# Attention and a state-space layer side by side: loads, masks, the skip term and the flag rearranged

## The chip, the cores and the metric

The kernel runs on one core of a Trainium2 chip. Five engines work beside each other: TensorE (matrix products), VectorE, ScalarE (written ACT), GpSimd and SyncE (SP), and DMA queues move data. The metric is the time of one execution on the device in microseconds; less is better.

## The reference

Two layers work on sequences of 2048 positions of width 448, and their outputs stand side by side in the result.

- Layer A is attention with 16 heads of width 28. Position s sees itself and seven earlier positions at distances 2, 4, ..., 14:

```
qkv    = x @ wqkv                              # q, k, v: 16 heads of 28
idx    = pos[:, None] - arange(8) * 2          # masked where idx < 0
attn   = softmax(q . k[idx] * 28**-0.5)
a      = (attn . v[idx]) @ wo
```

- Layer B is a linear recurrence with a complex diagonal of 448 entries:

```
dt = exp(log_dt);  Lam_bar = exp(dt * Lam)
B_bar = ((Lam_bar - 1) / Lam)[:, None] * (B_re + i B_im)
h[t] = Lam_bar * h[t-1] + B_bar @ x[t]
y[t] = 2 * real(C @ h[t]) + x[t] * Dskip
out  = concatenate([a, y], axis=-1)            # bf16, 1 x 2048 x 896
```

The term `x * Dskip` is called the skip term below.

## The kernel before

**Two positions as one.** All distances in layer A are even, so even and odd positions never meet. The kernel reads both inputs as 1024 pairs of width 896, transposed on the way in (`xA`, `xB`: pieces of 128 pairs, the helper `xbar_x`, lines 277 and 278). Layer B is also run on pairs: the scan has 1024 steps, and the odd and the even output of a pair are two products.

**Loads.** Lines 284 to 303 issue the loads. SP issues the transposing loads of x and then those of B. ACT issues the three parts of `wqkv`: V into `Wv`, K and Q into `Wraw`, each in a part of 384 rows and a tail of 64 rows. GpSimd issues the four small vectors of layer B into `rows`. A DMA takes one of eight semaphores in turn, so a ninth load waits on its issuing engine until the load that had its semaphore before has landed.

**Layer A.** `v0` to `v8` (name in the plan) are the projections to V, each in two halves of 4 and 3 pairs of matmuls on the two halves of TensorE's rows (`pair`, line 509). Between the halves stands a tiny memset on GpSimd, the tick (`relay`, line 523): it waits for the first half, and the second half waits for it. `wp` (`n_wp`, line 481) copies K and Q weights into the padded `Wpad`; `q<q><s><c>` are the projections to K and Q in three chunks of positions. `s`, `x`, `a`, `n`, `ot` are scores with mask (`msk`, built on GpSimd by `gms`, lines 324 to 336), exponentials on ACT (line 690), weighted sums of V (line 702), normalization on VectorE (line 709) and a transpose by DMA into `OT`. `w0` to `w7` multiply with `wo` and are stored.

**Layer B.** `tr`, `pA`, `pB`, `e1`, `e2`, `p2`, `p3` compute the small per-entry coefficients from `rows`; `p3` (line 455) is a chain of 26 and more VectorE operations of 128x4 elements that gives the coefficients that scale C. `t0` to `t4` make tables of sines and cosines (`tab`): `t0` and `t1` (line 433) the arguments, `t2` and `t4` the sines on ACT. The exponentials of layer A wait for `t4`. `l1`, `l2`, `wtx` scale B and transpose it by DMA into `WT`; `b<half><k>` multiply with x (line 742); then on VectorE `ma`, `ri`, `sc`, `mb`, `ro`: rotate by the tables, scan, rotate back into the state `h`. `cg`, `ch` scale C into `C1` and `C2`, `g` makes `Gm`. `y0` to `y7` (the even outputs, line 879 and 881) and `z0` to `z7` (the odd outputs, lines 888 to 891) are the output products for 128 pairs each; y4 to y7 need the second half of the scan. The skip term of the even output is inside `Gm` (by the diagonal `dgE`); that of the odd output is four matmuls with the diagonal matrices `dgO` (lines 889 and 891).

**The guard.** The softmax leaves out the maximum. `guard1` to `guard3` (lines 932 to 945) test that every sum stayed within bounds and write `flag`. At the end every engine loads the flag (line 956) and branches (line 958) to `exact_attention`, which runs only if the test fails.

**Order.** Each step above is a node of a plan (class `Plan`, line 33): with the engines that may run it and an estimated cost for each, what it depends on, a rank, and for some an earliest time `at`. `run` is a greedy list schedule on these estimates: an engine that is free takes the ready node of the lowest rank. Ranks come from the table `RANK` (line 27), two numbers for a group: a start and a step per index. The result is a fixed order of instructions on each engine, which the chip then follows, with semaphores between engines. PSUM is held by four units (`unit`), each taken by a product and given back by its eviction (`evac`, line 491, on VectorE or ACT).

Of the kernel before, what the change touches and what calls it, by code (L numbers as in the profile page):

```python
# [7 lines left out]
BF16 = mybir.dt.bfloat16  # L8
# [8 lines left out]
NB = 9  # L17
# [9 lines left out]
RANK = {"v": (-66.31, 15.076), "q0": (294.15, -25.592), "q1": (-315.77, 68.252), "s": (340.5, 1.243), "a": (-235.18, 100.084), "b0": (313.86, 16.665),  # L27
        "b1": (1356.35, 1.953), "d0": (322.12, 89.775), "d1": (1443.2, 48.596), "l": (1449.65, 70.241), "t": (88.82, 72.345), "p3": (-158.67, -158.858),
        "cg": (19.42, -10.986), "ch": (1359.74, -129.532), "g": (444.15, -19.668), "y": (337.07, 51.059), "w": (1219.89, 24.257), "gu": (1542.4, -111.348),
        "q2": (576.66, 87.15), "wp": (286.96, 21.742)}  # L30
# [186 lines left out]
def kernel(  # L217
# [65 lines left out]
    V.memset(zz[:, 0:640], 0.0)  # L283
    xbar_x(xA, xA2, 0, 128)
    ACT.dma_start(Wv[:, 0:3, :], A_wqkv[0:384, 2 * D:3 * D].rearrange("(k p) n -> p k n", p=128))
    ACT.dma_start(Wv[0:64, 3, :], A_wqkv[384:448, 2 * D:3 * D])
    for i, vec in enumerate((B_log_dt, B_Lambda_re, B_Lambda_im, B_Dskip)):
        G.dma_start(rows[7 * i:7 * i + 7, :], vec.rearrange("(c p) -> c p", p=64))
    for i in range(1, 4):
        xbar_x(xA, xA2, 128 * i, 128 * i + 128)  # L290
    for q in (1, 0):
        ACT.dma_start(Wraw[:, 0:3, D * q:D * q + D], A_wqkv[0:384, D * q:D * q + D].rearrange("(k p) n -> p k n", p=128))
        ACT.dma_start(Wraw[0:64, 3, D * q:D * q + D], A_wqkv[384:448, D * q:D * q + D])
    for i in range(4, 8):
        xbar_x(xA, xA2, 128 * i, 128 * i + 128)
# [6 lines left out]
    for i in range(4):  # L302
        xbar_x(xB, xB2, 128 * i, 128 * i + 128)
# [129 lines left out]
    def n_t1(e):  # L433
        for k in range(4):
            kk = tmpB[:, 2560 + 512 * (k % 2):3072 + 512 * (k % 2)]
            V.tensor_scalar(kk, iota, p["f2"][:, k:k + 1], MAGIC, ALU.mult, ALU.add)
            V.scalar_tensor_tensor(ang[:, k, :], kk, -MAGIC, ang[:, k, :], ALU.add, ALU.subtract)  # L437
# [17 lines left out]
    def n_p3(e):  # L455
        q = {k: v[:] for k, v in p.items()}
        ts(q["nr"], q["a1"], -1.0, ALU.add)
        tt(q["den"], lre, lre, ALU.mult); tt(q["t0"], lim, lim, ALU.mult); tt(q["den"], q["den"], q["t0"], ALU.add)
        V.reciprocal(q["rd"], q["den"])
        ts(q["rd"], q["rd"], 2.0, ALU.mult)  # L460
        tt(q["gr"], q["nr"], lre, ALU.mult); tt(q["t0"], q["b1"], lim, ALU.mult)
        tt(q["gr"], q["gr"], q["t0"], ALU.add); tt(q["gr"], q["gr"], q["rd"], ALU.mult)
        tt(q["gi"], q["b1"], lre, ALU.mult); tt(q["t0"], q["nr"], lim, ALU.mult)
        tt(q["gi"], q["gi"], q["t0"], ALU.subtract); tt(q["gi"], q["gi"], q["rd"], ALU.mult)
        tt(q["hr"], q["gr"], q["a1"], ALU.mult); tt(q["t0"], q["gi"], q["b1"], ALU.mult); tt(q["hr"], q["hr"], q["t0"], ALU.subtract)
        tt(q["hi"], q["gr"], q["b1"], ALU.mult); tt(q["t0"], q["gi"], q["a1"], ALU.mult); tt(q["hi"], q["hi"], q["t0"], ALU.add)
        for n in ("g", "h"):
            re, im, sa, pa = q[n + "r"], q[n + "i"], q["s" + n], q["p" + n]
            ts(sa[:, 0:3], re[:, 0:3], 1.0, ALU.mult)
            tt(sa[:, 3:4], re[:, 3:4], sgn[:], ALU.mult)  # L470
            ts(sa[:, 4:7], re[:, 0:3], -1.0, ALU.mult)
            ts(pa[:, 0:4], im[:, 0:4], -1.0, ALU.mult)
            ts(pa[:, 4:7], im[:, 0:3], -1.0, ALU.mult)
# [71 lines left out]
    def halves(name, cost, fn, deps, rank, h, at):  # L545

        x = node(name + "_", {"P": 4 * cost}, lambda e: fn(0), deps, rank, alloc="mm", at=at, mode="h")
        k = node(name + "k", {"G": 0.12}, lambda e: relay(h), [x], -200)
        return x, node(name, {"P": 3 * cost}, lambda e: fn(1), [k], -50, mode="h")
# [4 lines left out]
    late = 17.0  # L554
    gm = []
    for i, f in enumerate(gms):
        gm.append(node(f"gm{i}", {"G": 0.42}, f, gm[-1:], 4, at=late))
# [4 lines left out]
    tr = node("tr", {"P": 0.15}, n_tr, [g_e], 0, alloc="mm", at=7.4)  # L562
# [8 lines left out]
    p3 = node("p3", {"V": 3.45}, n_p3, [p2], ("p3", 0))  # L571
    t0 = node("t0", {"A": 2.4}, n_t0, [pB, g_i], ("t", 0))
    t1 = node("t1", {"V": 4.6}, n_t1, [t0], ("t", 0))
    t2 = node("t2", {"A": 1.9}, n_t2, [t1, e2], ("t", 0))
    t3 = node("t3", {"V": 1.2}, n_t3, [t2], ("t", 0))
    t4 = node("t4", {"A": 2.0}, n_t4, [t3], ("t", 0))
    dg = [node(f"dgO{k}", {"G": 0.5}, lambda e, k=k: g_dgO(e, k), [pD], 15, at=late) for k in range(4)]
    for k in range(4):
        dg.append(node(f"dgE{k}", {"G": 0.5}, lambda e, k=k: g_dgE(e, k), [pD] + gm + dg[4:], 15, at=late))
    vw = node("vw", {"V": 1.0}, n_vw, [], 0, at=5.3)  # L580
    wp = {(q, z): node(f"wp{q}{z}", {"V": 1.55, "A": 2.9}, lambda e, q=q, z=z: n_wp(e, q, z), [g_p], ("wp", 2 * z + 1 - q), at=8.5 if q else 10.0)
# [19 lines left out]
    for i, m in enumerate(MS):  # L601
        h = {}
        l1 = node(f"l1{m}", {"A": 0.58, "V": 0.46}, lambda e, m=m, h=h: n_l1(e, m, h), [p2], ("l", i), alloc="wt", at=16.8)
# [22 lines left out]
    def at_x(t):  # L626
        return (5.9, 6.9, 7.8, 8.9, 10.2, 11.5, 12.8, 14.1)[(t - 1) // 128]
# [104 lines left out]
    for hf in range(2):  # L732
        for k in range(4):
# [45 lines left out]
            def ro(e, k=k, hf=hf, h=h, big=big):  # L779
# [8 lines left out]
                else:  # L788
                    V.tensor_tensor(hb[0:64, 3, to], a[0:64, 0], a[64:128, 1], ALU.subtract)
                    V.tensor_tensor(hb[64:128, 3, to], a[64:128, 0], a[0:64, 1], ALU.add)  # L790
                    if hf == 0:
# [3 lines left out]
                      rb_, alloc="mm", at=22.5)  # L795
# [64 lines left out]
    outv = out[0].rearrange("(t two) n -> t two n", two=2)  # L860
    ny = [0]

    def stage():
        if "ys" not in lazy:
            lazy["ys"] = t_([128, 8, 2, D], BF16, "ys", "rW")
        ny[0] += 1
        return lazy["ys"][:, (ny[0] - 1) % 8]
    for t in range(8):
        tk = slice(128 * t, 128 * t + 128)
        hf = t // 4  # L870
        h = {}

        def pe0(e, t=t, tk=tk, h=h, hf=hf):
            if t == 6:
                tc.mark_branch_hint_location("exact", engines=(mybir.EngineType.PE,))
            ps = h[0] = h[1] = unit()
            hb, lo = hbuf(hf), 128 * (t % 4)
            for m in range(7):
                PE.matmul(ps[:, 0, 0:D], hb[:, m, lo:lo + 128], lazy["C2"][:, m, :], start=(m == 0), stop=False, skip_group_check=True)  # L879
            for k in range(4):  # L880
                PE.matmul(ps[:, 0, 0:D], xB[:, k, tk], Gm[:, k, :], start=False, stop=(k == 3), skip_group_check=True)  # L881

        def pe1(e, t=t, tk=tk, h=h, hf=hf):
            if t == 7:
                h[1] = unit()
            ps, hb, lo = h[1], hbuf(hf), 128 * (t % 4)
            for m in range(7):
                PE.matmul(ps[:, 1, 0:D], hb[:, m, lo + 1:lo + 129], lazy["C1"][:, m, :], start=(m == 0), stop=False, skip_group_check=True)  # L888
            PE.matmul(ps[:, 1, 0:64], xB[:, 3, tk], dgO[:, 0, 0:64], start=False, stop=False, skip_group_check=True)
            for k in range(3):  # L890
                PE.matmul(ps[:, 1, 64 + 128 * k:192 + 128 * k], xB[:, 4 + k, tk], dgO[:, 1 + k, :], start=False, stop=(k == 2), skip_group_check=True)  # L891

        def ev(e, a, b, h=h):
            if "o" not in h:
                h["o"] = stage()
            evac(e, h["o"][:, a:b], h[a][:, a:b, 0:D])

        def st(e, a, b, tk=tk, h=h):
            SP.dma_start(outv[tk, a:b, D:2 * D], h["o"][:, a:b])
        r = ("y", t)  # L900
        hs = [rout[hf, k] for k in range(4)]
        n0 = node(f"y{t}", {"P": 2.0}, pe0, hs + c2 + gn, r, alloc="mm")
        n1 = node(f"z{t}", {"P": 1.57}, pe1, [n0] + c1, (r[0], r[1], -0.1), alloc="mm" if t == 7 else None)
        for a, b in ((0, 1), (1, 2)) if t == 7 else ((0, 2),):
            n2 = node(f"ye{t}{a}", ab((b - a) * D), lambda e, a=a, b=b, ev=ev: ev(e, a, b), [n1 if b == 2 else n0] + qdone, r,
                      frees=[(n1 if a else n0, 0)])
            node(f"yo{t}{a}", {"S": 0.6}, lambda e, a=a, b=b, st=st: st(e, a, b), [n2], 60 + 3 * t, lat=2.2)
    for t in range(8):
        tk = slice(128 * t, 128 * t + 128)
        h = {}  # L910

        def pe(part, tk=tk, h=h):
            if part == 0:
                h["ps"] = unit()
            o, w = OT(), lazy["wo"]
            pair(h, part, h["ps"], D, lambda o_, k: o[o_:o_ + 64, k, tk], lambda o_, k: w[o_:o_ + 64, k, :])

        def ev(e, h=h):
            h["o"] = stage()
            evac(e, h["o"], h["ps"][:, :, 0:D])  # L920
# [69 lines left out]
```

## Time and profile before

| | us |
|---|---|
| median of 7 runs | 138.84 (138.62 to 140.29) |
| profiled execution | 138.76 |
| its span | 136.9 |
| TensorE busy (matmul) | 127.4 |
| VectorE busy | 104.6 |
| ScalarE busy | 93.0 |
| GpSimd busy | 21.5 |

The span runs from the first to the last recorded instruction of the program; the execution is 1.9 us longer. Busy time counts the time in which an engine works, without waits and without issuing DMAs. The page also cuts the span into 40 slices of 3.42 us and gives the busy share of each in tenths. "PE" is TensorE, "PEld" its loading of weights, "DVE" VectorE, "POOL" GpSimd, and a "q" behind a name means the engine's sequencer. In a row of the timeline stand start, length, engine, line, operation, what is written and read, the count, and in brackets how long the engine had been idle and what ended that.

### The profile page before, as it was taken

To read this page: it belongs to the slowest core of one execution; us is meant where nothing else is said; L and a number is where in the kernel's file an instruction comes from. 1 tells how busy PE (TensorE), PEld (TensorE's weight loads), DVE (VectorE), ACT (ScalarE), POOL (GpSimd) and SP (SyncE) were. 2 spreads that over 40 slices of the span, in tenths; PEclk is the share of its full clock that TensorE was granted. 3 is DMA by queue.
4 is the path that set the end of the run, shared out by engine and by line. 5 is a ranking of instruction groups with operands and counts; after the bars stand their busy time and mean duration, and the time that the engine had idled before them with its cause. 6 is when DMAs were issued, how large, how long until landed. Compare 5 with 4: busy or idle time off the path is not lost.

```text
span 136.9 us, 3790 instructions
## 1 busy us (share of the span) xinstructions
PE 127.4 (93%) x1536; PEld 71.6 (52%) x1542; DVE 104.6 (76%) x222; ACT 93.0 (68%) x123; POOL 21.5 (16%) x85
## 2 busy tenths in 40 slices
PE   6669999999999999979999999999999999999970
PEld 2224666897443454545455464655565655455540
DVE  0546986999996999999999999999999999500000
ACT  0174969996999579699999879935775267322230
POOL 6500148889400000000000000000000000000000
PEclk9999999999999999999999999999999999999999
DMA  3999999500668899142201106099222478541121
GB/s 75 263 260 232 245 137 203 92 0 5 118 127 164 118 242 192 38 90 57 59 0 24 39 0 66 6 258 101 59 72 74 117 45 257 168 139 67 67 101 43
DMA packets 42372, 15.13 MB, mean 111 GB/s; under 512 B 34992, under 2 KB 42352, under 8 KB 42352
## 3 DMA queue, kind: packets, MB, share of 16 engines
q1 hardware_dynamic: 40784, 13.65, 49.3%
q10 hardware_dynamic: 1440, 1.20, 3.2%
q8 instruction: 13, 0.21, 0.7%
q14 instruction: 7, 0.06, 0.1%
q0 software_dynamic: 128, 0.00, 0.1%
HBM read 3.16 MB, written 3.67 MB: 50 GB/s over the span
## 4 chain that ended last, share of the span: by engine, by line
PE 68%; DVE 11%; ACT 10%; DMA 5%; issue 2%; SPq 1%; DVEq 0%; ACTq 0%
PE mm L516 18%; PE mm L742 14%; PE mm L879 8%; PE mm L888 8%; PE mm L702 5%; DMA xA<-in_A_x_dram 5%; PE mm L881 4%; PE mm L839 4%; PE mm L680 3%; ACT P L690 3%; PE mm L684 2%; DVE tmpB L437 2%; DVE Vt L495 2%; ACT tab L446 1%; ACT tab L440 1%
## 5 line engine op out<-in xcount | busy, mean ns | idle before, releaser
L690 ACT ACTIVATE P<-mm 128x896 bf16<-128x896 f32 (+1 forms) x36 | 31.3, 932 | 4.0 <-PE mm L684 3.9
L516 PE MATMUL mm<-xA,Wpad 64*128 64x256 bf16 (+1 forms) x168 | 26.7, 305 | 0.3 <-ACT P L690 0.3
L493 ACT CAST ys<-mm 128x896 bf16<-128x896 f32 (+1 forms) x16 | 13.5, 861 | 20.0 <-PE mm L891 13.9
L517 PE MATMUL mm<-xA,Wpad 64*128 64x256 bf16 (+1 forms) x168 | 26.8, 305 | 0.0
L742 PE MATMUL mm<-xB,WT 128*128 128x512 bf16 x92 | 22.2, 380 | 0.5 <-ACT P L690 0.2
L524 POOL MEMSET tick<- 1x1 f32 x41 | 5.3, 129 | 93.8 <-PE mm L517 93.4
L516 PEld LDWEIGHTS <-Wpad 64*128 64x128 bf16 x168 | 15.1, 94 | 7.8 <-POOL tick L524 0.6
L516 PE MATMUL mm<-Wv,xA 64*128 64x448 bf16 x63 | 13.5, 350 | 2.5 <-DMA xA<-in_A_x_dram 2.5
L517 PEld LDWEIGHTS <-Wpad 64*128 64x128 bf16 x168 | 14.8, 94 | 0.8 <-issue 0.7
L742 PEld LDWEIGHTS <-WT 128*128 128x128 bf16 x98 | 9.0, 97 | 11.3 <-issue 1.0
L517 PE MATMUL mm<-Wv,xA 64*128 64x448 bf16 x63 | 13.5, 350 | 0.0
L879 PE MATMUL mm<-C,h 128*128 128x448 bf16 x56 | 11.9, 352 | 0.2 <-ACT P L690 0.2
L888 PE MATMUL mm<-C,h 128*128 128x448 bf16 x56 | 11.9, 353 | 0.0
L517 PE MATMUL mm<-wo,OT 64*128 64x448 bf16 x56 | 10.8, 349 | 0.0
L516 PE MATMUL mm<-wo,OT 64*128 64x448 bf16 x56 | 10.8, 349 | 0.0
L945 DVE TENSOR_SCALAR flag<-mm 1x1 int32<-1x1 f32 x1 | 0.1, 145 | 13.5 <-PE mm L942 13.5
L709 DVE TENSOR_TENSOR O<-mm,rcs 112x896 bf16<-112x896 f32 (+1 forms) x9 | 9.8, 1091 | 0.3
L516 PEld LDWEIGHTS <-xA 64*128 64x128 bf16 x63 | 5.5, 94 | 7.9 <-DMA xA<-in_A_x_dram 3.7
L702 PEld LDWEIGHTS <-P 128*128 128x128 bf16 x288 | 8.2, 96 | 1.5 <-issue 0.8
L493 ACT CAST Qt<-mm 128x512 bf16<-128x512 f32 (+1 forms) x10 | 7.5, 760 | 2.0 <-PE mm L517 2.0
L702 PE MATMUL mm<-Vt,P 128*128 128x29 bf16 x288 | 8.7, 176 | 0.0
L776 DVE TENSOR_TENSOR_SCAN rs<-p_r,ini,rv 128x512 bf16<-128x512 f32 x7 | 8.6, 1268 | 0.0
(174 smaller groups left out, 240.0 us busy)
## 6 DMA issues: line engine op xcount, KB each, us to landing
out_dram<-ys SPq DMA_DIRECT2D x15, 224.0 KB, 2.4
Wraw<-in_A_wqkv_dram ACTq DMA_DIRECT2D x2, 336.0 KB, 5.8
wo<-in_A_wo_dram SPq DMA_DIRECT2D x2, 336.0 KB, 4.1
Wv<-in_A_wqkv_dram ACTq DMA_DIRECT2D x1, 336.0 KB, 3.6
natW<-in_B_B_re_dram SPq DMA_DIRECT2D x1, 336.0 KB, 4.1
natW<-in_B_B_im_dram SPq DMA_DIRECT2D x1, 336.0 KB, 5.1
out_dram<-ys SPq DMA_DIRECT2D x2, 112.0 KB, 1.7
OT<-O SPq DMA_TRANSPOSE x9, 2.8
```

The costliest lines, as they stand in the source:

```text
L493: ACT.copy(o, i)
L516: x = PE.matmul(ps[:, a, 0:n], lhs(0, lo[i]), rhs(0, lo[i]), start=(i == 0), stop=(i == 6), skip_group_check=True)
L517: y = PE.matmul(ps[:, b, 0:n], lhs(64, hi[i]), rhs(64, hi[i]), start=(i == 0), stop=(i == 6), skip_group_check=True)
L690: ACT.activation(P[:].rearrange("p s g q -> p g s q")[:, 2 * z:2 * z + 2, :, 0:n], h["s"][z][:, :, 0:4 * n].rearrange("p g (s q) -> p g s ...
L702: PE.matmul(av[:, par, 29 * hd:29 * hd + 29], hb_[par]["P"][:, hd // 4, hd % 4, :], Vt[:, par, b, hd, :], start=True, stop=True)
L709: V.tensor_tensor(O[0:n, :].rearrange("p (a h d) -> p a h d", a=2, h=H), avv[0:n, :, :, 0:DH], rc.unsqueeze(3).to_broadcast((n, 2, H, DH)) ...
L742: PE.matmul(ps[:, i, :], WT[:, j, 128 * m:128 * m + 128], xB[:, j, HALF * hf:HALF * hf + HALF], start=(j == 0), stop=(j == 6))
L776: V.tensor_tensor_scan(h["s"][:, i], p["r2"][:, k:k + 1].to_broadcast((128, HALF)), h["v"][:, i], 0.0 if hf == 0 else ini[:, m:m + 1], ALU ...
L839: PE.matmul(ps[0:n, i, 0:D], natW[:, m, D + 128 * k:D + 128 * k + n], lazy["C1"][:, m, :], start=(m == 0), stop=False, skip_group_check=True)
L879: PE.matmul(ps[:, 0, 0:D], hb[:, m, lo:lo + 128], lazy["C2"][:, m, :], start=(m == 0), stop=False, skip_group_check=True)
L881: PE.matmul(ps[:, 0, 0:D], xB[:, k, tk], Gm[:, k, :], start=False, stop=(k == 3), skip_group_check=True)
L888: PE.matmul(ps[:, 1, 0:D], hb[:, m, lo + 1:lo + 129], lazy["C1"][:, m, :], start=(m == 0), stop=False, skip_group_check=True)
```

## The change

1. **Loads.** The tails of Q and K come by one load from ACT, right behind V's. The main parts of K and Q are written behind x pieces 1 to 3 and behind pieces 4 and 5. The load of `B_Lambda_re` goes from GpSimd to ACT. xB's first half comes in two pieces of 256 pairs instead of four of 128.
2. **GpSimd.** The fifteen mask steps `gm` lose their earliest time (17 before) and so come ahead of the rest of GpSimd's work. The other steps get 18 or 45.
3. **Coefficients.** `p3` is split: three products and a reciprocal stay on VectorE (`p3a`), and 26 operations become single GpSimd nodes `p3b0` to `p3b25`, at 37 or later.
4. **Tables.** `t1` is split into eight nodes; the four first steps (`tk`) no longer wait for `t0`.
5. **Skip term.** For y4, y5 and y6 the four `dgO` matmuls go. Instead the odd rows of x and Dskip are loaded once (`xn`, after the last scores), multiplied on VectorE (`xd`), and added on VectorE as the odd output is taken from PSUM; these blocks are stored as one, after that addition.
6. **Order of the end.** y5 to y7 wait for all w blocks; the last odd output is taken from PSUM in two halves, on ACT and VectorE; the guard's matmul waits for z7.
7. **Flag.** It is loaded without bounds, so without an assertion.
8. **Plan.** New `RANK` numbers, costs, earliest times and engine start times.

The core of the diff:

```diff
-    for i, vec in enumerate((B_log_dt, B_Lambda_re, B_Lambda_im, B_Dskip)):
+    ACT.dma_start(Wraw[0:64, 3, :], A_wqkv[384:448, 0:2 * D])
+    for i, vec in ((0, B_log_dt), (2, B_Lambda_im), (3, B_Dskip)):
         G.dma_start(rows[7 * i:7 * i + 7, :], vec.rearrange("(c p) -> c p", p=64))
     for i in range(1, 4):
         xbar_x(xA, xA2, 128 * i, 128 * i + 128)
-    for q in (1, 0):
-        ACT.dma_start(Wraw[:, 0:3, D * q:D * q + D], A_wqkv[0:384, D * q:D * q + D].rearrange("(k p) n -> p k n", p=128))
-        ACT.dma_start(Wraw[0:64, 3, D * q:D * q + D], A_wqkv[384:448, D * q:D * q + D])
-    for i in range(4, 8):
+    ACT.dma_start(rows[7:14, :], B_Lambda_re.rearrange("(c p) -> c p", p=64))
+    ACT.dma_start(Wraw[:, 0:3, D:2 * D], wmain(1))
+    for i in range(4, 6):
+        xbar_x(xA, xA2, 128 * i, 128 * i + 128)
+    ACT.dma_start(Wraw[:, 0:3, 0:D], wmain(0))
+    for i in range(6, 8):
         xbar_x(xA, xA2, 128 * i, 128 * i + 128)
...
-    for i in range(4):
-        xbar_x(xB, xB2, 128 * i, 128 * i + 128)
+    xbar_x(xB, xB2, 0, 256)
+    xbar_x(xB, xB2, 256, 512)
...
-        gm.append(node(f"gm{i}", {"G": 0.42}, f, gm[-1:], 4, at=late))
+        gm.append(node(f"gm{i}", {"G": 0.45}, f, gm[-1:], 4))
...
-    p3 = node("p3", {"V": 3.45}, n_p3, [p2], ("p3", 0))
+    p3 = node("p3a", {"V": 0.5}, n_p3a, [pA], 1.7)
+    for i, f in enumerate(p3b()):
+        p3 = node(f"p3b{i}", {"G": 0.35}, f, [p3] if i else [p3, p2], 4, at=37.0)
...
-    t1 = node("t1", {"V": 4.6}, n_t1, [t0], ("t", 0))
-    t2 = node("t2", {"A": 1.9}, n_t2, [t1, e2], ("t", 0))
+    tss = []
+    for k in range(4):
+        tk_ = node(f"tk{k}", {"V": 0.53}, lambda e, k=k: n_tk(e, k), [pB, g_i] + (tss[k - 2:k - 1] if k > 1 else []), ("tk", k))
+        tss.append(node(f"ts{k}", {"V": 0.62}, lambda e, k=k: n_ts(e, k), [t0, tk_], ("t", 0)))
+    t2 = node("t2", {"A": 1.9}, n_t2, tss + [e2], ("t", 0))
...
+    YD = (4, 5, 6)
+    def n_xn(e):
+        xo = sk["x"] = t_([128, 4, D], BF16, "xo", "Kt")
+        SP.dma_start(xo[:, 0:3, :], B_x[0].rearrange("(b t two) d -> t b two d", two=2, t=128)[:, YD[0]:YD[2] + 1, 1, :])
+        SP.dma_start(xo[:, 3, :], B_Dskip.partition_broadcast(128))
+    xl = node("xn", {"S": 1.2}, n_xn, sdone, 25, lat=3.0)
+    def n_xd(e, i):
...
+        V.tensor_tensor(sk["d"][:, i, :], sk["x"][:, i, :], sk["x"][:, 3, :], ALU.mult)
...
-                PE.matmul(ps[:, 1, 0:D], hb[:, m, lo + 1:lo + 129], lazy["C1"][:, m, :], start=(m == 0), stop=False, skip_group_check=True)
+                PE.matmul(ps[:, 1, 0:D], hb[:, m, lo + 1:lo + 129], lazy["C1"][:, m, :], start=(m == 0), stop=(t in YD and m == 6), skip_group_check=True)
+            if t in YD:
+                return
...
+        elif t in YD:
+            def add(e, t=t, h=h):
+                V.tensor_tensor(h["o"][:, 1], h[1][:, 1, 0:D], sk["d"][:, t - YD[0], :], ALU.add)
...
+            n3 = [node(f"ye{t}{1 + i}", {"AV"[i]: 0.3}, lambda e, i=i, half=half: half(e, 224 * i, 224 * i + 224), [n1, n2], r, frees=[(n1, 0)])
+                  for i in range(2)]
...
-    bad = nc.values_load(flag[0:1, 0:1], min_val=0, max_val=128)
+    bad = nc.values_load(flag[0:1, 0:1])
```

## The prediction

> **What bounds the kernel now.** I read the page's busy shares first, then TensorE over the stretches, then the first ten microseconds and the last four of the timeline.
>
> ```profile
> PE 127.4 (93%) x1536; PEld 71.6 (52%) x1542; DVE 104.6 (76%) x222; ACT 93.0 (68%) x123; POOL 21.5 (16%) x85
> DVE  0546986999996999999999999999999999500000
> GB/s 75 263 260 232 245 137 203 92 0 5 118 127 164 118 242 192 38 90 57 59 0 24 39 0 66 6 258 101 59 72 74 117 45 257 168 139 67 67 101 43
> ```
>
> TensorE is nearly full, and VectorE is nearly full too between slice 7 and slice 33, then has nothing to do. So there are two clocks. TensorE must get through its list, and VectorE must deliver the second half of the scan before block y4 can start. The stretches show how close each is (length, then busy time of PE, PEld, DVE, ACT, POOL):
>
> ```profile
> 6.50:8.81 2.31, 0.93 (x8) 0.31 (x9) 0.39 (x1) 1.75 (x2) 0.09 (x1) 1.00 1.30 194
> 37.50:44.00 6.50, 6.27 (x55) 2.50 (x53) 5.21 (x9) 6.47 (x7) 0.11 (x1) 1.00 0.79 151
> 57.50:60.50 3.00, 2.31 (x52) 1.28 (x50) 2.93 (x8) 2.37 (x3) 0.00 (x0) 1.00 0.23 45
> 117.20:132.80 15.60, 15.59 (x101) 8.20 (x95) 1.09 (x1) 4.23 (x6) 0.06 (x1) 1.00 0.31 105
> ```
>
> TensorE loses 1.4 us before 8.81 and under 2 us in all the rest, mostly around 43 and 59 us. VectorE's last scan output ends at 117.18 (timeline) and y4 starts at 118.11, so VectorE has 0.9 us to spare. From there to the end it is matmuls alone. Any gain must therefore come from the head, from fewer matmuls, or from the tail.
>
> **Head.** Timeline, start and length:
>
> ```profile
> 5.10 0.81 DVE L478 COPY Wv<-Wv 64x1344 bf16<-64x1344 bf16 x1
> 5.94 0.50 DVE L479 COPY Wv<-Wv 64x1344 bf16<-64x1344 bf16 x1
> 6.53 0.36 PE L516 MATMUL mm<-Wv,xA 64*128 64x448 bf16 x1 [1.10 <-DMA xA<-in_A_x_dram]
> 8.81 0.36 PE L516 MATMUL mm<-Wv,xA 64*128 64x448 bf16 x1 [1.35 <-DMA xA<-in_A_x_dram]
> ```
>
> The first V block starts at 6.53, when the first x piece has landed (6.48) and the V weights are copied (6.44). Its first half, 4 pairs at 0.19, ends by 7.3. TensorE then stands in front of x piece 2 until 8.81, while the second half of block v0 (3 pairs, 0.57 us) is queued behind. Pieces 1 to 4 land at 6.48, 8.76, 10.32, 11.50. The K load is issued at 1.88 between them.
>
> After the change only V's weights (401 KB), the 115 KB tail of Q and K and x pieces 1 and 2 (229 KB each) are wanted first: 974 KB. The page's first two slices of 3.42 us moved 75 x 3.42 + 263 x 3.42 = 1157 KB by 6.85 us. At that rate 974 KB are through at about 6.2 us, and piece 2 should land near 7.3 instead of 8.76. The start stays near 6.5, because the copy on L479 sets it as well. v0 and v1 (14 pairs x 0.19 = 2.66 us) then end at 9.2; before, that amount was reached at about 10.7. K now lands later. If pieces 3 and 4 (0.9 us of transfer each at 0.25 MB per us) and then K's copies (1.6 us on VectorE) come in time, all 1.5 us are kept; if K's 344 KB push piece 3 back to where it was, 0.3. I take **-1.0 us**, ends -1.6 and +0.3. K's delay, from 8.9 to about 10, must be covered by blocks v2 and v3 (2.66 us); without them TensorE waits about 1 us. The tail of Q and K costs ACT one issue of about 0.5 us instead of two. The Lambda_re load goes from GpSimd's queue (0.52 us off it) to ACT's, 0.5 us. ACT has no work before K arrives, and its next customer, the Wpad copies, waits for the same loads. Two xB issues take the place of four at 1.30 to 1.68 us each on SP; behind them SP waits 10 us for VectorE anyway (34.22), so I cost this at nothing.
>
> **Matmuls removed.** Blocks y4, y5, y6 lose one L889 and three L891 matmuls each.
>
> ```profile
> 131.01 1.49 PE L888 MATMUL mm<-C,h 128*128 128x448 bf16 x7
> 132.33 0.19 PE L889 MATMUL mm<-dgO,xB 128*128 128x64 bf16 x1
> 132.36 0.33 PE L891 MATMUL mm<-dgO,xB 128*128 128x128 bf16 x3
> 132.73 0.53 ACT L493 CAST ys<-mm 128x448 bf16<-128x448 f32 x1 [0.94 <-PE mm L891]
> 133.29 0.36 SPq L899 DMA_DIRECT2D out_dram<-ys  x1
> ```
>
> In the timeline the last L888 of y4 starts at 121.34 and the next block at 121.72, 0.38 us; without the four the pitch is 0.19. That is **-0.6 us** for three, in the stretch where nothing but TensorE counts. In exchange VectorE does three multiplies (nearest row L755, 128x1024 bf16, 0.69; so about 0.5 each) and three additions from PSUM (L709 takes 1.09 for 896 columns, so 0.55 each). VectorE is idle from 117.2 for 13 us apart from one eviction, so both are covered if the multiplies sit behind the last scan; in front of it they would eat 1.5 us against 0.9 us of slack. Their load (344 KB plus the Dskip row to all partitions, two SP issues of about 0.55) goes after the last scores, 102.8 us here; a 336 KB load took 4.1 us to land, so 107 to 108 against a need at about 119. The stores of y4 to y6 now wait for the addition; behind them on SP stands only the next store. y5 to y7 wait for all w blocks, which stand ahead of them already. The new load may delay an OT transpose: the one issued at 89.95 beside the wo load took 5.3 us instead of 2.8. w0 to w7 have 10.7 us of other work for that.
>
> **Tail.** The queue's entries of the last lines (duration, first and last start):
>
> ```profile
> L956 SPq TENSOR_LOAD <-flag x1: 532/532/532, 133.7 to 133.7; - x1
> L956 SPq FUSED_REGOPS  x1: 192/192/192, 134.3 to 134.3; - x1
> L956 SPq SEQ_ASSERT  x1: 29/29/29, 134.5 to 134.5; - x1
> L958 SPq COMPARE_BRANCH  x1: 58/58/58, 134.6 to 134.6; - x1
> ```
>
> SP issues the last store at 133.29, then works through these one after another, and its closing waits run from 134.8 without a pause although the store lands at 135.00. The end at 136.9 hangs on SP's sequence. Without FUSED_REGOPS and SEQ_ASSERT the branch comes 0.07 after the load, as it does on ACT, instead of 0.39: -0.32. If the register operations stay, -0.08. The last eviction (0.53 on ACT, 448 columns) becomes two halves side by side; ACT's rows 0.91 for 896 and 0.53 for 448 give 0.35 for 224, so -0.18. Together **-0.5 us**.
>
> **Middle.** The 26 small operations of p3 leave VectorE, where they stand from 24.7 to 28.5 ahead of the table's arguments; about 0.6 us (three products and the reciprocal) stay, and the tk steps can run while VectorE waits. The tables, at 41.25 now, can come some 3 us earlier, and VectorE gets 3 us of slack. TensorE has at most 2 us of holes there. The new ranks reorder all engines, and that order can't be read from this trace; I assume that it fills TensorE as well as the old one and count **0**, ends -0.8 and +1.5. The cost is on GpSimd, and here a rule speaks against the change. GpSimd's rows:
>
> ```profile
> L330 POOL TENSOR_TENSOR mst<-mst 32x128 bf16<-32x128 bf16 x1 | 0.4, 417 | 0.1
> L307 POOL TENSOR_SCALAR_AFFINE_SELECT dgO<-dsr 128x128 bf16<-128x128 bf16 x4 | 2.6, 653 | 0.0
> L307 POOL TENSOR_SCALAR_AFFINE_SELECT eye<-eye 128x128 bf16<-128x128 bf16 x1 | 0.3, 288 | 0.1
> ```
>
> The nearest row for a 128x4 operation is the 0.417 of 128 elements as the upper end, and the 0.09 of the tick memset as the lower. The Trainium skill (SBUF — State Buffer, Who interferes with whom) says that VectorE and GpSimd share a port pair as an exclusive lock, and that a VectorE instruction with two SBUF inputs and a GpSimd instruction that reads SBUF block each other for its whole length. The trace agrees: the select of 128x128 takes 0.29 alone and 0.65 beside a full VectorE, and L478 takes 0.81 beside GpSimd's iota where L479, same shape, takes 0.50. By the rows alone the chain is 26 x 0.2 = 5 us in GpSimd's idle time after 37; by the rule each one may wait for a VectorE operation of about 0.4, 26 x 0.6 = 16 us, and hold VectorE 26 x 0.15 = 4 us. Either is over before the first C scaling at 64 us, so GpSimd's lateness itself costs nothing. What is queued behind it is the tick that releases each second half of a projection block; the plan gives an operation 0.35. I take 0.25. The masks in the head do the same to K's copies, five copies by at most 0.3.
>
> **Sum.** -1.0 - 0.6 - 0.5 + 0 = -2.1. The profiled execution took 138.76 with a span of 136.9; the same 1.9 us outside it leaves 134.8 + 1.9 = 136.7. The median shown is 138.84, 0.1 above that execution, so **136.7 us** stands for both.
>
> **Rivals.** (1) The head gives back what it gained: TensorE starts earlier but then waits for K, or VectorE's locked port eats the slack and y4 waits as before. Left are 0.6 + 0.5: 137.7. For it speaks that 0.26 MB per us is all that the queues moved; against it, that V work is at hand. (2) Slower: the ticks queue behind the p3 chain. TensorE's loss is the greatest lateness, 26 x (actual - 0.35). At the upper row with a wait, 0.5, that is 3.9 us, so 138.8 - 2.1 + 3.9 = 140.6. It passes the old time from 0.43 us per operation on. For it: the 0.65 selects; against it: four elements instead of 128, and few ticks after 37 us (five until 63 us). (3) A new order, written by changed ranks, puts the weight transposes (VectorE's l steps from 33.5, first WT at 37.25) behind other work; TensorE runs out of projections at 37.7 less 1.0 and waits about 1.5 us. 138.2.
>
> **Numbers.** Forecast 0.62, rival 1 0.17, rival 2 0.12, rival 3 0.09. A measurement here tells 0.5% (0.7 us) from no change. Forecast and most of rival 1 are faster: 0.78; rival 3 and the rest are the same: 0.10; rival 2: 0.12. The likeliest case has 135.4 to 137.6 (head and middle at their ends); over the cases 135.3 to 138.8.
>
> **What would show it.** Second V block near 7.8 and no hole after 9.5; y4 to y7 at 3.4 us a block; no SEQ_ASSERT; VectorE done with the scan before TensorE asks for y4. Wrong if TensorE waits for the tick, for Wpad or for WT, or if y4 waits for VectorE.

## The result and the profile after

The changed kernel takes 137.7 us (median of 26 runs, 137.16 to 140.05) against 138.84 (median of 63 in the same comparison). The ratio is 0.9911, with a 95% interval of 0.9892 to 0.9929: faster by 0.9%, some 1.2 us. In the profiled executions the span falls from 136.94 to 135.85 us, by 1.09. The forecast was 136.7, with 135.3 to 138.8 as its range: the direction and the range hold, the gain is a little over half of the 2.1 us expected.

The page of the changed kernel, busy time and two of its rows over 40 slices of 3.4 us:

```profile
PE 126.9 (93%) x1525; PEld 69.9 (51%) x1530; DVE 109.6 (81%) x204; ACT 89.7 (66%) x122; POOL 28.9 (21%) x110
DVE  0519999999989899999999999999999999911110
GB/s 94 251 247 277 283 173 182 76 2 107 111 149 155 165 154 153 36 64 59 0 35 29 0 0 64 170 130 68 55 79 120 159 114 232 176 135 72 68 101 43
```

TensorE's share is as it was. VectorE has 5 us more to do; its last slices are no longer empty, because the additions of y4 to y6, 0.62 us each, stand there. GpSimd rose by 7.4 us.

The same stretches as before (length, busy time of PE, PEld, DVE, ACT and POOL, then granted clock, DMA share and GB/s); the first and last now begin and end where the corresponding matmuls do:

```profile
6.11:8.10 1.99, 0.93 (x8) 0.31 (x10) 0.00 (x0) 0.00 (x0) 1.80 (x8) 1.00 1.23 207
37.50:44.00 6.50, 5.94 (x61) 2.68 (x59) 6.10 (x10) 5.05 (x6) 6.34 (x19) 1.00 0.83 148
57.50:60.50 3.00, 3.00 (x69) 1.85 (x67) 2.93 (x6) 2.86 (x5) 0.00 (x0) 1.00 0.36 70
117.72:131.80 14.08, 14.08 (x79) 7.32 (x77) 2.97 (x4) 2.67 (x6) 0.00 (x0) 1.00 0.29 97
```

The head still has a hole in front of the second V block, now of 1.06 us. The hole near 59 us is gone; around 40 us there is more idle time than there was. From y4 on TensorE is busy without a gap, while VectorE works for 2.97 us beside it, 1.09 of them one eviction and the rest the three additions: these are covered.

Timeline of the head (start, length):

```profile
4.66 0.81 DVE L490 COPY Wv<-Wv 64x1344 bf16<-64x1344 bf16 x1
5.50 0.50 DVE L491 COPY Wv<-Wv 64x1344 bf16<-64x1344 bf16 x1
6.11 0.36 PE L528 MATMUL mm<-Wv,xA 64*128 64x448 bf16 x1 [0.81 <-DMA xA<-in_A_x_dram]
8.10 0.36 PE L528 MATMUL mm<-Wv,xA 64*128 64x448 bf16 x1 [1.06 <-DMA xA<-in_A_x_dram]
```

V starts 0.42 us earlier than before (6.53), the second V block 0.71 earlier (8.81). Pieces 1 to 4 of x landed at 6.07, 8.05, 9.46 and 9.99, where they had landed at 6.48, 8.76, 10.32 and 11.50; K landed at 9.26.

Timeline of the tail:

```profile
131.35 0.19 PE L974 MATMUL mm<-dgO,xB 128*128 128x64 bf16 x1
131.38 0.33 PE L976 MATMUL mm<-dgO,xB 128*128 128x128 bf16 x3
131.64 0.16 PE L897 MATMUL mm<-okb,one 128*1 128x1 bf16 x1
131.75 0.35 ACT L505 CAST ys<-mm 128x224 bf16<-128x224 f32 x1 [0.94 <-PE mm L976]
132.12 0.39 DVE L507 CAST ys<-mm 128x224 bf16<-128x224 f32 x1 [2.75 <-ACT ys L505]
```

The two halves of the last eviction do not run side by side. VectorE's half names ScalarE's as what it waited for, and starts 0.02 us after its end. SP's queue behind the last store, by line (shortest, median and longest duration in ns, first and last start):

```profile
L1014 SPq TENSOR_LOAD <-flag x1: 533/533/533, 132.9 to 132.9; - x1
L1016 SPq COMPARE_BRANCH  x1: 58/58/58, 133.5 to 133.5; - x1
```

FUSED_REGOPS and SEQ_ASSERT are gone, and the branch follows the load directly.

**A table for all kernels.** The execution falls into stages that can be read to a few hundredths: the second V block (it starts 0.04 to 0.05 us after x piece 2 has landed), the first matmul of y4, the small guard matmul that follows the last block, the issue of the last store, and the end. All times are us, one profiled execution each.

| kernel | x piece 2 landed | second V block | from there to y4 | y4 to guard | guard to last store | store to end | end |
|---|---|---|---|---|---|---|---|
| before | 8.76 | 8.81 | 109.30 | 14.51 | 0.67 | 3.65 | 136.94 |
| after | 8.05 | 8.10 | 109.62 | 13.92 | 0.90 | 3.31 | 135.85 |
| after, on the chip of the first experiments | 7.95 | 8.00 | 109.61 | 13.93 | 0.90 | 3.31 | 135.75 |
| after, last eviction in one piece | 8.07 | 8.11 | 109.62 | 13.93 | 0.66 | 3.30 | 135.62 |
| after, dgO matmuls back | 7.75 | 7.80 | 109.68 | 14.51 | 0.91 | 3.30 | 136.20 |
| after, old loads | 8.53 | 8.58 | 109.75 | 13.92 | 0.90 | 3.32 | 136.47 |
| before, no assertion | 8.88 | 8.93 | 110.71 | 14.51 | 0.66 | 3.33 | 138.14 |
| before, new loads | 7.46 | 7.50 | 109.43 | 14.51 | 0.66 | 3.64 | 135.74 |
| after, p3 on VectorE | 7.98 | 8.02 | 110.14 | 13.92 | 0.91 | 3.29 | 136.28 |
| after, K and Q on SP's queue | 7.82 | 7.87 | 111.24 | 13.92 | 0.90 | 3.31 | 137.24 |
| after, masks at 17 us | 7.45 | 7.50 | 111.45 | 13.92 | 0.90 | 3.31 | 137.08 |
| the same, one piece | 7.97 | 8.02 | 111.45 | 13.92 | 0.67 | 3.31 | 137.37 |
| the same, two PSUM tiles | 7.40 | 7.45 | 111.46 | 13.94 | 0.60 | 3.31 | 136.76 |
| before, new loads, masks at 5 us | 7.48 | 7.52 | 109.91 | 14.51 | 0.66 | 3.64 | 136.24 |

The first two rows give the whole account: -0.71 in the head, +0.32 in the middle, -0.59 in the y blocks, +0.23 in the last eviction, -0.34 behind the store, together -1.09. The execution of the kernel before without the assertion had a mean granted TensorE clock of 0.988 where before and after had 1.0 and 0.993 (matmuls at half pace between 8.9 and 11.7 us), so only its last two stages are compared.

The stages repeat where the landing of x piece 2 does not. With the new loads on ScalarE's queue the piece landed anywhere from 7.40 to 8.07 in ten executions, and that spread goes into every timed median; the intervals of the ratios below are 0.7 to 1.1% wide. So the verdict on an edit is read from its stage first, and the timed ratio stands beside it.

### The profile page after: what moved, and what is told of

It is laid out like the page before. It is cut to its first block, busy times and chain, and to the rows that moved or that the text cites. A ratio compares the mean times of both kernels' runs of the same rounds, so it can differ in the third digit from the quotient of the medians.

```text
span 135.9 us, 3784 instructions
## 1 busy us (share of the span) xinstructions
PE 126.9 (93%) x1525; PEld 69.9 (51%) x1530; DVE 109.6 (81%) x204; ACT 89.7 (66%) x122; POOL 28.9 (21%) x110
## 4 chain that ended last, share of the span: by engine, by line
PE 75%; ACT 15%; DMA 4%; SPq 1%; issue 1%; DVE 0%; ACTq 0%
PE mm L528 23%; PE mm L764 14%; PE mm L962 8%; PE mm L971 8%; PE mm L724 6%; PE mm L964 4%; DMA xA<-in_A_x_dram 4%; PE mm L861 4%; PE mm L702 4%; PE mm L706 3%; ACT Wpad L501 2%; ACT Wpad L500 2%; ACT tab L454 1%; ACT P L712 1%; ACT Wpad L497 1%; ACT tmpB L436 1%
## 5 line engine op out<-in xcount | busy, mean ns | idle before, releaser
L505 ACT CAST ys<-mm 128x896 bf16<-128x896 f32 (+2 forms) x15 | 11.3, 771 | 19.1 <-PE mm L971 8.9
L507 DVE CAST Vt<-mm 128x896 bf16<-128x896 f32 x6 | 6.4, 1085 | 3.7 <-PE mm L529 3.6
L996 DVE TENSOR_TENSOR ys<-mm,xd 128x448 bf16<-128x448 f32 x3 | 1.9, 625 | 8.5 <-ACT ys L505 8.5
L798 DVE TENSOR_TENSOR_SCAN rs<-p_r,rv 128x512 bf16<-128x512 f32 x7 | 8.5, 1221 | 0.0
```

What stands on the lines that cost most here:

```text
L505: ACT.copy(o, i)
L507: V.tensor_copy(o, i)
L798: V.tensor_tensor_scan(h["s"][:, i], p["r2"][:, k:k + 1].to_broadcast((128, HALF)), h["v"][:, i], 0.0 if hf == 0 else ini[:, m:m + 1], ALU ...
```

## The experiments

**The changed kernel again**, as a measure for the three runs that follow.

> The changed kernel once more, as the measure for the runs beside it. Every theory: 1.0 to 1.3 us under the kernel before.

Measured: ratio to before 0.9884 (0.9828 to 0.9939), median 138.05 against 139.48. Its stages agree with those of the first profile to 0.02 us; only piece 2 landed 0.1 us earlier.

**The last eviction in one piece.**

```diff
-n3 = [node(..., half(e, 224 * i, 224 * i + 224), [n1, n2], ...) for i in range(2)]
+n3 = [node(..., half("A", 0, 448) if i == 0 else None, [n1, n2], ...) for i in range(2)]
```

> The changed kernel with the last 448 columns evicted in one piece on ScalarE instead of in halves on ScalarE and VectorE. Theory: in the changed kernel VectorE's half starts only when ScalarE's is over, so that from the last matmul to the store's issue it takes 0.83 us against 0.58 before; one piece takes 0.58 again, and the kernel is 0.25 us faster than the changed one. Rival (the halves run side by side, and something else made the tail late): 0.1 to 0.2 us slower than the changed one.

Measured: ratio to before 0.9840 (0.9795 to 0.9886), median 137.31, on the same chip as the control's 138.05. From guard to store 0.66 us instead of 0.90. The timeline:

```profile
131.76 0.53 ACT L505 CAST ys<-mm 128x448 bf16<-128x448 f32 x1 [0.94 <-PE mm L976]
132.32 0.34 SPq L984 DMA_DIRECT2D out_dram<-ys  x1
```

One 0.53 us eviction beats 0.35 and 0.39 in a row. The theory holds in its place and size (0.24); the rest of the difference between the two medians is within their intervals. It has the lowest median of all versions measured here, but its interval overlaps the control's, so that the stage is what shows the gain.

**The dgO matmuls back** (the skip term is then counted twice in three blocks).

```diff
-                ..., stop=(t in YD and m == 6), skip_group_check=True)
-            if t in YD:
-                return
+                ..., stop=False, skip_group_check=True)
```

> The changed kernel with the four dgO matmuls back in each of blocks y4 to y6, the additions on VectorE left in (the skip term is then counted twice in three blocks). Theory: TensorE alone sets the time there, 3 x 0.19 us: 0.6 us slower than the changed one. Rival (the additions or the stores hold the blocks as well, so that the matmuls were in part covered): 0 to 0.3 us slower.

Measured: y4 to guard 14.51 us, to the hundredth what it was before the change. The ratio, 0.9895 (0.9848 to 0.9943), cannot show the loss beside the control's. The end is only 0.45 us later than the control's because piece 2 landed 0.20 earlier. In that stage TensorE alone counts: 12 matmuls, 0.59 us.

**The old loads under the new order.** The load section is that of before; what the engines do and in which order stays.

> The changed kernel with the loads of x, weights and vectors in the order of before; the order of work on the engines stays that of the changed kernel. Theory: the loads gave TensorE 0.4 us at its start and some of it survives the projections: 0.3 to 0.7 us slower than the changed one. Rival (the lead of the head is eaten up by 46 us, where TensorE stands 1.8 us behind the kernel before, and the end is set by what comes later): 0.0, within 0.1.

Measured: second V block at 8.58 instead of 8.00 in the control, end at 136.47 instead of 135.75. So 0.58 us in the head are 0.72 at the end; nothing is given back on the way. The ratio, 0.9904 (0.9862 to 0.9946), and the median, 138.14 beside the control's 138.05, do not separate it from the control. That the loads move piece 2 is clear of its spread: in the three profiles with the old loads it landed between 8.53 and 8.88, in ten with the new ones between 7.40 and 8.07. The rival rested on a trap: in the middle of the run the changed kernel seemed far behind, because its order brings other work forward. Progress counted in matmuls can't be compared between two orders before both reach the same block.

**The assertion alone taken away.**

```diff
-    bad = nc.values_load(flag[0:1, 0:1], min_val=0, max_val=128)
+    bad = nc.values_load(flag[0:1, 0:1])
```

> The kernel before with one edit: the load of the flag carries no bounds, so no assertion. Theory: SP's chain after the last store sets the end, FUSED_REGOPS and SEQ_ASSERT leave it: 0.33 us faster than the kernel before. Rival (the end hangs on the landing of the last store): 0.0.

Measured: store to end 3.33 us instead of 3.65. The timed ratio, 0.9974 (0.9929 to 1.0018), agrees with the 0.33 us expected and with nothing at all; the stage is what shows it, as do the rows with and without the assertion: 3.64 and 3.65 in three, 3.29 to 3.33 in eleven.

**The new loads alone** in the kernel before.

> The kernel before with one edit: the loads of the changed kernel; the order of work on the engines stays that of before. Theory after the run with the old loads: the loads are worth 0.5 to 0.6 us whatever the order, and nothing behind the head takes it back: 0.5 us faster than the kernel before. Rival (K comes later than the old order wants it, so TensorE waits for Wpad): 0.0 to 0.5 us slower.

Measured: ratio 0.9904 (0.9864 to 0.9944), median 137.63: some 1.3 us where 0.5 was expected. The head in the timeline:

```profile
6.30 0.36 PE L520 MATMUL mm<-Wv,xA 64*128 64x448 bf16 x1 [0.47 <-DMA xA<-in_A_x_dram]
7.50 0.36 PE L520 MATMUL mm<-Wv,xA 64*128 64x448 bf16 x1 [0.27 <-DMA xA<-in_A_x_dram]
```

The second V block comes 1.31 us earlier than in the kernel before, y4 1.18 earlier. The theory (next to no give-back) holds; its size was too small, because it took the landing at 8.05 for the loads' fixed effect. That raised a new question: why does piece 2 land at 7.46 here and near 8.0 in the changed kernel with the same loads?

**p3 on VectorE**, in the places that the 26 operations have in the new order.

```diff
-        return lambda e: G.tensor_tensor(o, a, b, op)
+        return lambda e: V.tensor_tensor(o, a, b, op)
```

(and the same for `tensor_scalar`)

> The changed kernel with the 26 small p3 operations at the same places of the plan on VectorE instead of GpSimd. Theory: VectorE must deliver the scan before y4 and has 1.9 us to spare in the changed kernel (last scan output 115.85, y4 from 117.72); the 26 operations cost it some 3.5 us, so y4 starts 1.0 to 1.7 us later and the kernel is that much slower. Rival (VectorE waits often enough for others between 37 and 115 us to take them in): within 0.2 us of the changed kernel.

Measured: y4 0.52 us later, counted from the second V block; ratio 0.9923 (0.9883 to 0.9963). The 26 operations took 4.06 us of VectorE, against 8.19 of GpSimd in the changed kernel. Neither theory is right in its mechanism. VectorE still finishes the scan 1.75 us ahead of y4, exactly as in the changed kernel (1.76). By the stage it is slower; the timed ratios of the two overlap. What is lost is lost in one place, where TensorE waits for the normalization that VectorE has not reached (timeline):

```profile
47.50 1.02 PE L764 MATMUL mm<-xB,WT 128*128 128x512 bf16 x4 [0.46 <-DVE O L731]
```

The matmuls are 0.62 us further apart there than their columns take, and in the changed kernel they are not; the delay then travels to the end unchanged. The time between the last scan output and y4 is therefore no slack that could be spent: both engines wait for one another on the way, and a delay of one moves both.

**K and Q on SP's own queue**, K behind piece 2 and Q behind piece 5.

```diff
-    ACT.dma_start(Wraw[:, 0:3, D:2 * D], wmain(1))
+    xbar_x(xA, xA2, 128, 256)
+    SP.dma_start(Wraw[:, 0:3, D:2 * D], wmain(1))
 ...
+    SP.dma_start(Wraw[:, 0:3, 0:D], wmain(0))
```

> The changed kernel with K's load issued on SP's own queue behind x piece 2 and Q's behind x piece 5, in place of ScalarE's queue. Theory: in the changed kernel K's packets still run beside x piece 2, which lands at 8.05; really behind it, x piece 2 lands near 7.3 and the hole in front of the second V block falls from 1.2 us to 0.5: 0.4 to 0.7 us faster than the changed kernel. Rival: K lands a microsecond later and its Wpad copies with it, TensorE waits there instead: 0.0 to 0.5 us slower.

Measured: the edit did not take K's load out of the way of piece 2. SP issued it right behind piece 2, at 3.51 us, where ScalarE issues it at 4.17 in the changed kernel; it landed at 8.28 instead of 9.26, so it was again under way beside piece 2, and earlier. Piece 2 landed at 7.82, inside the spread of the others. In this one execution K's load, 0.66 us sooner, did not make piece 2 late; whether piece 2 would be earlier without K beside it stays open, because K was under way in every run. What did change is that the x pieces behind Q's load come late (piece 6 landed at 15.09 instead of 12.74), and TensorE stands in front of them for 1.6 us from 13.6 on. The two waits for x in the head, in the list of waits (total, times, longest):

```profile
PE mm L527 <- DMA xA<-in_A_x_dram: 2.3, 2, 1.6
```

From the second V block to y4 it takes 1.62 us more. The ratio of 0.9886 (0.9832 to 0.9940) does not show that loss: the profiled execution was the slowest of its seven (138.95, the others 137.21 to 137.97), so the loss is that of one execution and may not be typical.

**The masks at 17 us**, where they were before; the other four engines keep the order of the changed kernel, operation for operation.

```diff
-        order.sort(key=lambda n: n["start"])
+        order.sort(key=lambda n: n["start"] + (14.0 if n["name"][:2] == "gm" else 0))
```

> The changed kernel with GpSimd's mask operations (msk, mst) at the time of before, some 17 us on, instead of 5 to 12.6; the order on the other four engines is that of the changed kernel, operation for operation. Theory (the masks are what holds x piece 2 back: with the same loads it landed at 7.46 in the old order and at 7.75 to 8.07 in five profiles of the new one, and the masks are the only work of another engine between 5.5 and 8 us that the two orders do not share): piece 2 lands near 7.5, the hole in front of the second V block falls from 1.0 to 0.4 us, 0.5 us faster than the changed kernel. Rival (chance or another cause): landing 7.8 to 8.1, 0.0.

Measured: piece 2 at 7.45 as the theory had it, and yet the kernel is slower than the changed one: ratio 1.0013 (0.9980 to 1.0046), the whole gain gone. From the second V block to y4 it takes 111.45 us instead of 109.62. GpSimd's timeline and, below it, the row in TensorE's list of waits (total, times, longest) show where:

```profile
19.06 0.93 POOL L312 TENSOR_SCALAR_AFFINE_SELECT mst<-mst 32x128 bf16<-32x128 bf16 x2
19.94 0.37 POOL L348 MEMSET P<- 128x256 bf16 x1
20.28 0.41 POOL L331 TENSOR_TENSOR msk<-mst 32x128 bf16<-32x128 bf16 x1
20.65 0.36 POOL L536 MEMSET tick<- 1x1 f32 x2
```

```profile
PE mm L528 <- POOL tick L536: 2.1, 4, 0.9
```

The tick that TensorE waits for from 20.1 on stands behind two selects, a memset and a product. In the changed kernel the same row reads

```profile
PE mm L528 <- POOL tick L536: 0.3, 1, 0.3
```

The 1.8 us more of this wait match the 1.83 us lost. This is rival 2 of the prediction, ticks behind GpSimd's small work, with another work in front. The new order needs the masks out of the way before 17 us.

**The same with the last eviction in one piece.**

> The run with the masks at 17 us and, in addition, the last eviction in one piece on ScalarE. Theory: the two gains add, 0.5 + 0.2: 0.7 us faster than the changed kernel, near 136.9. Rival (masks no cause): 0.2 faster, near 137.4.

Measured: ratio 1.0019 (0.9982 to 1.0055). Piece 2 landed at 7.97 this time, with the masks still late and everything ahead of the tail as in the run before. That refutes the theory on the masks. The tail gives 0.23 us again (0.67 against 0.90).

**The old order, new loads, masks early** (the same shift in the sort, by -11.5 us, in the kernel with the new loads alone).

> The kernel before with the new loads and with GpSimd's masks early, from about 5.5 us; the order on the other engines is that of before. Theory (masks hold x piece 2 back): piece 2 lands near 8.0 instead of 7.46, 0.5 us slower than the same kernel with the masks late, near 138.1. Rival (the early part of the order of another engine makes the difference): piece 2 near 7.5, 137.6 as with the masks late.

Measured: ratio 0.9984 (0.9942 to 1.0025). Piece 2 landed at 7.48 beside the early masks, the second refutation. Slower it is all the same, for another reason: from the second V block to y4 109.91 us instead of 109.43. K's weight copies on VectorE run beside GpSimd's masks, and the first of them takes, in the list of what writes the weight tile (durations in ns, first and last start),

```profile
L489 DVE COPY Wpad<-Wraw x1: 573/573/573, 8.7 to 8.7; 128x672 bf16<-128x672 bf16 x1
```

where with the masks late it took

```profile
L489 DVE COPY Wpad<-Wraw x1: 394/394/394, 8.7 to 8.7; 128x672 bf16<-128x672 bf16 x1
```

The copy on L492 takes 508 ns instead of 390. The five copies end 0.4 us later, and the V evictions behind them start 0.4 us later. That this 0.4 is the 0.48 at y4 is likely, but no run separates it from the ticks behind the masks, for which TensorE waits 0.2 us here and not at all with the masks late. The twelve timed runs lie in groups near 137.9, 138.8 and 139.5; the profile is of the lowest, and what makes the others is not known.

**The last odd block in two PSUM tiles**, with the masks at 17 us: columns 0 to 191 in one, evicted on ScalarE while TensorE computes columns 192 to 447 in another, which VectorE evicts.

```diff
+            if t == 7:
+                h[2] = unit()
+                for b_, c0, c1, ks in ((1, 0, 192, (0,)), (0, 192, 448, (1, 2))):
+                    for m in range(7):
+                        PE.matmul((h[1] if b_ else h[2])[:, 1, c0:c1], hb[:, m, lo + 1:lo + 129], lazy["C1"][:, m, c0:c1], ...)
 ...
```

> The run with the masks at 17 us, with the last odd block in two PSUM tiles, columns 0 to 191 first and evicted on ScalarE, columns 192 to 447 after them and evicted on VectorE. Theory (the halves of the changed kernel follow one another because they read one PSUM tile): VectorE's part no longer waits for ScalarE, and takes 0.42 us after the last matmul; seven more matmuls and weight loads cost 0.1 to 0.3 us; so 0.2 us slower to 0.1 faster than the run with the masks at 17 us and one piece on ScalarE. Rival (the common output tile makes them follow): VectorE still waits for ScalarE's part.

Measured: ratio 0.9984 (0.9947 to 1.0021). The timeline of the tail:

```profile
132.65 0.28 PE L978 MATMUL mm<-dgO,xB 128*128 128x128 bf16 x2
132.85 0.16 PE L897 MATMUL mm<-okb,one 128*1 128x1 bf16 x1
132.96 0.42 DVE L507 CAST ys<-mm 128x256 bf16<-128x256 f32 x1 [2.38 <-PE mm L978]
```

VectorE's part waits for TensorE and no longer for ScalarE, though both still write the same output tile. So it is the common PSUM tile that puts the halves in a row: in the program as built VectorE's instruction carries a wait on ScalarE's, and it carries none when the tiles differ. Guard to store takes 0.60 us, 0.30 less than with the halves of the changed kernel and 0.07 less than with one piece. The seven more matmuls cost next to nothing (y4 to guard 13.94 against 13.92). This tail with the masks early wasn't run.

## Why the prediction was right, and where it was not

**Sum.** Forecast -1.0, -0.6, -0.5 and 0; measured in the two profiles -0.71, -0.59, -0.11 and +0.32. Of the missing 1.0 us the halves account for 0.41, the middle for 0.32 and the head for 0.29.

One comparison belongs beside this sum. The new loads alone reached a median of 137.63 and a ratio of 0.9904, no worse than the 137.7 and 0.9911 of the whole change. By the stages the rest of the change is worth 0.49 us on top of the loads (+0.19 in the middle, -0.59, +0.24, -0.33), but piece 2 landed at 7.46 there and at 8.05 in the changed kernel, which takes that back. Whether the new order itself makes piece 2 land later is not settled.

**Head, -1.0 with ends -1.6 and +0.3: right in mechanism and sign.** The second V block was to come near 7.3 to 7.8; it came at 8.10 in the profiled execution and between 7.45 and 8.11 in the ten executions with these loads on ScalarE's queue, that is 0.70 to 1.36 us earlier than before. The step took one landing time for the loads' effect, while the landings of these ten lie up to 0.67 apart. The start was not held at 6.5: V's first load landed 0.28 us earlier (4.15), so its copies ended at 6.00 and the first block began at 6.11. This part is not shown to come from the change: in two other runs with the old loads that load landed at 4.23 and 4.28. The assumption that K waits behind piece 2 was wrong, though K's load is written behind piece 4 (and Q's behind piece 6, counted from 1 as here): its issue waits only for V's first load, at 4.17, and K landed beside piece 3. What this costs piece 2 no run shows. The runs with the loads exchanged show that an early start is kept to the end, which refutes the mechanism of rival 1. Its time, 137.7, is what the runs gave, but by another way: 0.7 of the miss came from the tail and the middle.

**Matmuls removed, -0.6: right.** 14.51 to 13.92 us, and back to 14.51 with the matmuls. The multiplies and additions are hidden as argued; an addition takes 0.62 us instead of 0.55 and waits for ScalarE's eviction of the other half of the block, at no cost: from y4 on TensorE has no gap.

**Tail, -0.5: half right.** The assertion gave -0.34 for -0.32. The halves "side by side", costed at -0.18, were the failed step: +0.23. ScalarE's 0.35 was right, and VectorE's 0.39 is behind it, not beside it. The prediction looked at durations and not at what the second half waits for.

**Middle, 0 with ends -0.8 and +1.5: inside, at +0.32.** It holds parts that are each larger than their sum. In the new order the move of p3 to GpSimd is worth 0.5 us, and the early masks 1.8. What the rest of the order costs can't be told apart, because no run has the old order with p3 moved. Where the 0.32 goes is not settled either: from the second V block to y4 TensorE counts as idle for 1.60 us before and 1.68 after, and as busy for 107.70 and 107.94, so most of it lies in gaps too short to count as idle. Of the signs named for a wrong prediction one appeared: TensorE waited for a tick, once and for 0.3 us, and it also kept holes of 0.2 to 0.3 us after 9.5.

**The rule on the port.** The rows alone allowed 0.2 us an operation. By the rule of the Trainium skill (SBUF — State Buffer, Who interferes with whom), that a VectorE instruction with two SBUF inputs contends with a GpSimd instruction that reads SBUF, the prediction estimated up to 0.6. Measured: 0.31 on average (8.19 us for 26), where 0.25 was taken; the same operations take 0.16 on VectorE. The average hides two kinds. Seventeen took 0.18 to 0.24 us, and nine 0.37 to 0.68; each of the nine started beside a VectorE instruction on SBUF tiles and ended 0.05 to 0.09 us after it. One of each kind in the timeline:

```profile
35.92 1.22 DVE L507 CAST Qt<-mm 128x1024 bf16<-128x1024 f32 x1
36.90 0.20 POOL L466 TENSOR_TENSOR p_gi<-p_gi,p_t 128x4 f32<-128x4 f32 x1
37.06 0.67 DVE L621 SCALAR_TENSOR_TENSOR natW<-natW,p_a,wtmp 128x448 bf16<-128x448 bf16 x1
37.17 0.62 POOL L466 TENSOR_TENSOR p_gi<-p_gi,p_rd 128x4 f32<-128x4 f32 x1
```

Beside the cast, which reads PSUM, the GpSimd operation takes 0.20 us; beside the VectorE operation with two SBUF inputs it lasts until that one is over. So the trace agrees with the rule, and the 0.6 was too high because only nine of the 26 were held up like this. The pair L478 and L479, which the prediction counts as agreement, is no case of this rule: the copy has one input, and the iota reads no tile.

No tick stood behind the 26 operations (one at 34.34, the next at 52.67), so rival 2 did not happen in this place; the run with the late masks shows that its mechanism is real and costs 1.8 us. Rival 3 did not happen: the first weight transpose was issued at 24.4 us instead of 34.2.

## What to carry to other kernels

Two engines that evict parts of one PSUM tile can run one after the other: look at what the second waits for, and give each its own tile, or leave the eviction whole. Small work on an engine that also passes on signals must be costed by where the signals stand in that order: the same masks at another time took away the whole gain. After an experiment, look in the trace whether the edit moved what it was to move: K's load, meant to come later, was issued earlier. When one landing time varies from run to run, split the execution at fixed points and judge each edit by its own stage; such a stage repeats to 0.02 us where the median of a run does not to 0.5.

## What the runs showed that was not expected

- X piece 2 landed between 7.40 and 8.07 us in ten executions with the same loads. The three runs with the masks at 17 us differ only in the tail and had 7.45, 7.97 and 7.40. The masks do not decide it (7.48 with them early, 7.97 with them late); K's share is untested. The cause is open.
- The tail behind the last store is fixed to 0.04 us in each form: 3.64 or 3.65 with the assertion, 3.29 to 3.33 without.
- Seven more matmuls with their weight loads, at 192 and 256 columns instead of 448, cost TensorE 0.02 us.
